# A fixed order for a kernel's first tiles, x sums taken after the transpose, and GpSimd sums in pieces

## The chip, the cores and the metric

The kernel runs on one core of a Trainium2 chip. The time is device microseconds of one execution of the whole program, as the median of several runs; a lower one is better. The core has TensorE (PE, matmuls and transposes), VectorE (DVE), ScalarE (ACT), GpSimd (POOL), and SyncE (SP), which here only issues transfers. Each engine works through a queue of its own in order and waits for others by semaphores.

## The reference

All inputs are float32. x has 2048 rows of 1024.

```python
xn = (x - mean(x)) / sqrt(var(x) + 1e-5)
q, k, v = split(xn @ wqkv)                    # 32 heads of 32 columns each
phi = lambda t: where(t > 0, t + 1, exp(t)) + 1e-6
kv = sum over s of phi(k)[s]^T v[s];  z = sum over s of phi(k)[s]
s = ((phi(q) @ kv) / (phi(q) . z + 1e-6)) @ wo
g = silu((silu(xn @ w1) * (xn @ w3)) @ w2)    # w1, w3: 1024 x 3584; w2: 3584 x 1024
out = x + s * g
```

## The kernel before

Every float32 operand of a matmul is split into two float32r parts: `split` copies the high part on ScalarE (L83) and subtracts it on VectorE (L84). A product takes three matmuls of 128 x 512 per 128 rows of contraction: high x high, high x low, low x high (`mm3`, L92 to L94).

All large products are done in Strassen's form (Winograd's variant): seven products of quarter size in place of eight. The x side needs A11, A12, A22 and four sums S1 to S4 of the quarters, the weight side B11, B21, B22 and T1 to T4. x is taken in two halves h of 1024 rows, each in two chunks of 512 rows; a quarter is a chunk by half the columns.

In the first half, `prepare_first` loads the four tiles (128 rows each, xa) of the first chunk, normalises them, transposes them on TensorE and splits them into A11 and A12. `prepare_rest` loads the tiles xb of the second chunk, takes `moments` (statistics, a square root on ScalarE, and one refining step in small operations), normalises, and forms the sums in `combined`, on GpSimd, 128 x 512 each. The results are written over xa and xb and then transposed and split. Three early groups (keys 0, values 0, keys 1: `gemm` with early=True) multiply B11 with A11 and B21 with A12 before the sums exist. Their whole weights (wk, wv) are loaded into the buffers in which xa lay (tag "raw", two of them), so such a load waits until both tiles of an xa buffer have been transposed for good. Split weights and the fourth tile xb3 share a pool of eight buffers ("b").

While the first half is multiplied (keys, values, queries, then 14 pairs of gate and up with w1 and w3), background jobs run one step per product (`catch_up`): `prepare_next` prepares the second half's x, seven operands of each of four tiles, and stores them to DRAM; after it `weight_sums` forms the T sums of w2 on GpSimd (`sums_of`). The up group's end stores h from GpSimd's queue (L525) and forms the sums of h (`four_sums`), four GpSimd operations of 128 x 256 for each of two chunks, stored to hs_d by SyncE, in the last pair by GpSimd.

The order of instructions on each engine is set when the program is built: a scheduler with its own estimate of time interleaves the streams, within what data, buffers and `tc.issue_after` (a program-order edge behind a given instruction) allow.

Of the kernel before, what the change touches and what calls it, by code (L numbers as in the profile page):

```python
# [16 lines left out]
P = 128  # L17
C = 512
# [4 lines left out]
def tile_linear_attention_times_swiglu(  # L23
# [55 lines left out]
    def split(pair, src, bias=None):  # L79

        hi, lo = pair[:, 0], pair[:, 1]
        if bias is None:
            nc.scalar.copy(out=hi, in_=src)  # L83
            nc.vector.tensor_sub(out=lo, in0=src, in1=hi.bitcast(F32))  # L84
        else:
            nc.scalar.activation(hi, src, AF.Identity, bias=bias)
            nc.vector.scalar_tensor_tensor(lo, src, bias, hi.bitcast(F32), op0=ALU.add, op1=ALU.subtract)
# [36 lines left out]
    def moments(xs, dst):  # L124

        n = len(xs)
        bs = st.tile([P, n, 2, nc.vector.BN_STATS_DIM], F32, tag="bs", name="bs")
        v = st.tile([P, n], F32, tag="v", name="v")
        u = st.tile([P, n], F32, tag="u", name="u")
# [4 lines left out]
        y = dst[:, :, 1]  # L134
        nc.vector.tensor_scalar_add(v, y, 1e-5)
# [11 lines left out]
    def turn_into(A, b, i, name):  # L147

        for n, src in b.items():
            p_ = bank(f"t{n}{name}")  # L150
            for k in range(ND // 2):
                nc.tensor.transpose(p_[:, k * P:(k + 1) * P], src[:, k * P:(k + 1) * P], ident)
            split(A[n][:, :, :, i * P:(i + 1) * P], p_.rearrange("p (k s) -> p k s", k=ND // 2))
# [4 lines left out]
    def prepare_first(A, mom):  # L158

        xs = []  # L160
        for g in range(TH // 4):
            t = load_rows([(2 * g + e) * P for e in range(2)], f"xa{g}")
            for e in range(2):
                i = 2 * g + e
                xs.append(t[:, e])
# [5 lines left out]
    def prepare_rest(A, mom, i, t0):  # L171

        t1 = job_tile([P, D], f"xb{i}") if i < 3 else pb.tile([P, D], F32, tag="b", name=f"xb{i}")
        nc.sync.dma_start(out=t1, in_=x[C + i * P:C + (i + 1) * P, :])
        j = TH // 2 + i
        moments([t1], mom[:, j:j + 1])
        normalise(t1, mom[:, j])
        b = combined(t0, t1, small(f"S1x{i}"))
        yield
        turn_into(A, {n: b[n] for n in ("S2", "S3", "S1", "A22", "S4")}, i, f"0_{i}")  # L180
        yield

    def combined(t0, t1, s1):

        a11, a12, a21, a22 = t0[:, :C], t0[:, C:], t1[:, :C], t1[:, C:]
        nc.gpsimd.tensor_add(out=s1, in0=a21, in1=a22)
        nc.gpsimd.tensor_sub(out=a21, in0=a11, in1=a21)
        nc.gpsimd.tensor_sub(out=a11, in0=s1, in1=a11)
        nc.gpsimd.tensor_sub(out=a12, in0=a12, in1=a11)
        return {"S1": s1, "S3": a21, "S2": a11, "S4": a12, "A22": a22}  # L190

    def prepare_next(i):


        def turn(n, src):
            p_ = bank(f"t{n}1_{i}")
            for k in range(ND // 2):
                nc.tensor.transpose(p_[:, k * P:(k + 1) * P], src[:, k * P:(k + 1) * P], ident)
            o = pb.tile([P, 2, ND // 2, P], FR, tag="b", name=f"{n}o{i}")
            split(o, p_.rearrange("p (k s) -> p k s", k=ND // 2))  # L200
            nc.sync.dma_start(out=a_d[n][:, :, :, i * P:(i + 1) * P], in_=o.bitcast(F32))

        def steps(_):
            t0, t1, t2 = (job_tile([P, D], f"xn{i}_{e}") for e in range(3))
            for c, t in enumerate((t0, t1)):
                r0 = HS + c * C + i * P
                nc.sync.dma_start(out=t, in_=x[r0:r0 + P, :])
# [3 lines left out]
            moments([t0, t1], m)  # L211
            yield True
            yield True
            normalise(t0, m[:, 0])
            yield True
            normalise(t1, m[:, 1])
            yield True
            yield True
            turn("A11", t0[:, :C])
# [728 lines left out]
```

## Time and profile before

| | |
|---|---|
| Time, three runs | 2447.94 us median (2447.08 to 2451.15) |
| The profiled execution's own time | 2447.93 us |
| Its span, first to last instruction | 2446.1 us |
| Mean granted TensorE clock | 0.992 |
| Moved by DMA | 408.12 MB, mean 167 GB/s |
| Chain that ended last | PE 79%, DVE 11%, issue 4%, DMA 4%, ACT 2%, POOL 1% |

The profile is one execution. A line number names the source line that issued an instruction, a tile name the buffer it writes (out<-in), with buffer numbers left out. Busy time of TensorE counts overlapping matmuls once. A wait is the idle time of an engine ahead of an instruction, put down to the instruction that released it.

### The profile page before, as it was taken

What the parts mean: (1) busy time and instruction counts of PE and PEld (TensorE: products, weight loads), DVE (VectorE), ACT (ScalarE), POOL (GpSimd) and SP (SyncE); (2) the same over time, 40 slices, a digit from 0 to 9 for tenths busy, and PEclk for the clock granted to TensorE, in tenths of its full rate; (3) what the DMA queues carried; (4) which work ended last, traced back from release to release, by engine and by line L of the source; (5) the groups of instructions that cost most, each with busy time, mean ns of one, the idle gap of its engine ahead of it and who ended that gap; (6) DMA issues with size and microseconds to landing.
All of it is one profiled execution on the core that took longest, in us unless ns stands there. A gap on an engine that the chain in (4) does not pass through costs nothing.

```text
span 2446.1 us, 31065 instructions
## 1 busy us (share of the span) xinstructions
PE 2358.0 (96%) x10624; PEld 1941.1 (79%) x10624; DVE 1792.1 (73%) x2694; ACT 919.8 (38%) x1648; POOL 724.4 (30%) x873
## 2 busy tenths in 40 slices
PE   5999998999999999999999999999999999999998
PEld 4788887778888888888888888888787788787876
DVE  7654777797777765558878878887745776767798
ACT  4333543323333234445433233323423434343443
POOL 3000122264545310001235552354210032323244
PEclk9999999999999999999999999999999999999999
DMA  3112455575656491124355664566755554454588
GB/s 129 52 52 69 140 170 162 157 257 181 207 173 219 149 345 52 35 78 153 128 196 200 218 227 151 183 230 216 241 157 178 149 156 143 134 153 127 161 277 266
DMA packets 377423, 408.12 MB, mean 167 GB/s; under 512 B 19824, under 2 KB 307568, under 8 KB 377264
## 3 DMA queue, kind: packets, MB, share of 16 engines
q1 hardware_dynamic: 355248, 332.46, 43.2%
q0 software_dynamic: 22016, 73.68, 8.0%
q8 instruction: 83, 1.36, 0.2%
q14 instruction: 76, 0.62, 0.1%
HBM read 268.44 MB, written 137.63 MB: 166 GB/s over the span
## 4 chain that ended last, share of the span: by engine, by line
PE 79%; DVE 11%; issue 4%; DMA 4%; ACT 2%; POOL 1%; SPq 0%; DVEq 0%; ACTq 0%; POOLq 0%
PE dB L92 1%; PE dB L94 1%; PE cB L92 1%; PE dB L93 1%; PE cB L94 1%; PE cB L93 1%; PE kv L415 1%; PE aB L94 1%; PE aB L92 1%; PE aB L93 1%; DMA wpr<-wp_d 1%; DVE acc L865 1%; PE trk L382 1%; DMA rT2B<-wt_d 1%; DMA rA11B<-h_d 1%
## 5 line engine op out<-in xcount | busy, mean ns | idle before, releaser
L474 POOL DMA_DIRECT2D pq_d<-pq x32 | 17.5, 547 | 502.0 <-DVE pq L376 501.9
L525 POOL DMA_DIRECT2D h_d<-sg x112 | 61.5, 549 | 278.5 <-DVE sg L524 257.8
L792 POOL TENSOR_TENSOR acc<-acc,uB 128x512 f32<-128x512 f32 x25 | 41.9, 1676 | 158.4 <-DVE uB L790 158.4
L540 POOL TENSOR_TENSOR w<-w 128x256 f32<-128x256 f32 x28 | 27.8, 992 | 103.5 <-DMA w<-in_B_w 103.5
L509 POOL TENSOR_TENSOR qd<-qd 128x128 f32<-128x128 f32 x32 | 26.6, 832 | 104.2 <-DVE qd L650 100.6
L512 POOL TENSOR_TENSOR hs<-sg,hs 128x256 f32<-128x256 f32 x56 | 54.9, 981 | 2.1
L771 POOL TENSOR_TENSOR acc<-acc,uB 128x512 f32<-128x512 f32 x7 | 11.7, 1666 | 145.8 <-ACT uB L763 145.8
L856 POOL DMA_DIRECT2D s_d<-s x32 | 17.3, 540 | 122.5 <-DVE s L798 64.5
L383 ACT ACTIVATE kvr<-trk 128x512 f32<-128x512 f32 x32 | 19.1, 597 | 77.7 <-PE trk L382 77.5
L510 POOL TENSOR_TENSOR hs<-hs,sg 128x256 f32<-128x256 f32 x56 | 45.9, 820 | 0.0
L511 POOL TENSOR_TENSOR hs<-sg 128x256 f32<-128x256 f32 x56 | 42.8, 765 | 0.0
L509 POOL TENSOR_TENSOR hs<-sg,sg 128x256 f32<-128x256 f32 x56 | 42.0, 749 | 1.1
L92 PE MATMUL cB<-T,XA22B 128*128 128x512 f32 x87 | 35.0, 403 | 6.6 <-DVE acc L796 6.2
L794 POOL TENSOR_TENSOR acc<-acc,uB 128x512 f32<-128x512 f32 x25 | 40.1, 1604 | 0.0
L83 ACT CAST XS4B<-rS4B 128x384 fp32r<-128x384 f32 (+1 forms) x40 | 19.6, 490 | 53.2 <-PE cB L94 45.2
L807 DVE TENSOR_TENSOR acc<-cB,acc 128x512 f32<-128x512 f32 x25 | 17.2, 688 | 30.2 <-PE cB L94 30.2
L84 DVE TENSOR_TENSOR XS1B<-rS1B,XS1B 128x384 fp32r<-128x384 f32 (+1 forms) x40 | 37.2, 931 | 1.7 <-ACT XS1B L83 1.6
L863 ACT ACTIVATE acc<-acc 128x512 f32<-128x512 f32 x32 | 20.2, 632 | 47.2 <-DVE acc L798 14.1
L83 ACT CAST XA11B<-rA11B 128x384 fp32r<-128x384 f32 (+1 forms) x40 | 19.7, 493 | 45.8 <-PE dB L94 28.4
L83 ACT CAST XS1B<-rS1B 128x384 fp32r<-128x384 f32 (+1 forms) x40 | 19.7, 493 | 45.4 <-PE cB L94 26.5
L83 ACT CAST XS3B<-rS3B 128x384 fp32r<-128x384 f32 (+1 forms) x40 | 19.6, 491 | 43.7 <-PE bB L94 15.6
L92 PE MATMUL aB<-B,XA12B 128*128 128x512 f32 x87 | 34.1, 392 | 1.9 <-ACT uB L788 1.6
(5864 smaller groups left out, 8907.8 us busy)
## 6 DMA issues: line engine op xcount, KB each, us to landing
h_d<-sg POOLq DMA_DIRECT2D x112, 256.0 KB, 4.4
hs_d<-hs SPq DMA_DIRECT2D x104, 256.0 KB
qs_d<-qd POOLq DMA_DIRECT2D x32, 512.0 KB, 4.4
w<-in_B_w SPq DMA_DIRECT2D x56, 256.0 KB
wt_d<-w SPq DMA_DIRECT2D x28, 512.0 KB
pq_d<-pq POOLq DMA_DIRECT2D x32, 256.0 KB, 3.0
pqd<-pq_d SPq DMA_DIRECT2D x16, 512.0 KB
S<-a_dS SPq DMA_DIRECT2D x16, 512.0 KB
```

What stands on the lines that cost most here:

```text
L83: nc.scalar.copy(out=hi, in_=src)
L84: nc.vector.tensor_sub(out=lo, in0=src, in1=hi.bitcast(F32))
L92: nc.tensor.matmul(acc, lhsT=wh, rhs=ah, start=start, stop=False, skip_group_check=True)
L93: nc.tensor.matmul(acc, lhsT=wh, rhs=al, start=False, stop=False, skip_group_check=True)
L94: nc.tensor.matmul(acc, lhsT=wl, rhs=ah, start=False, stop=stop, skip_group_check=True)
L509: nc.gpsimd.tensor_add(out=s1, in0=a21, in1=a22)
L510: nc.gpsimd.tensor_sub(out=s2, in0=s1, in1=a11)
L511: nc.gpsimd.tensor_sub(out=s3, in0=a11, in1=a21)
L512: nc.gpsimd.tensor_sub(out=s4, in0=a12, in1=s2)
L525: nc.gpsimd.dma_start(out=h_d[i][2 * h + c][:, 2 * k + n], in_=sg[n, c])
L792: G.tensor_add(out=c22, in0=c22, in1=u)
L794: G.tensor_add(out=c12, in0=c12, in1=u)
```

## The change

1. `moments` has one small operation less, writes the square root to a tile of its own, and takes up to two tiles at a time.
2. `prepare_first` transposes and splits all four tiles of A11 first, then all of A12.
3. The second chunk's tiles are loaded in pairs with their statistics taken per pair (`load_second`). All of that, on each engine, is ordered behind the last split of A12 and behind the GpSimd sums of the tile before, so that the sums run tile by tile.
4. There are four early groups in place of three (values 1 is new), with a buffer of its own for the first group's partial result. The third and the fourth group's second product stand behind the transposes of tiles 0 and 1.
5. `prepare_next` transposes the four quarters and forms the sums from the transposed quarters on VectorE; per tile there are four groups of transposes where there were seven, no GpSimd operation where there were four of 128 x 512, four more VectorE operations and three more ScalarE copies. It needs two row buffers, not three, and 16 steps, not 17.
6. `four_sums` yields after each two operations, and in the first half each half of the sums is stored from GpSimd's queue as soon as it is there. `sums_of` yields after its first two operations, so a background job spreads it over two steps.

```diff
@@ split @@
-            nc.vector.tensor_sub(out=lo, in0=src, in1=hi.bitcast(F32))
+            return nc.vector.tensor_sub(out=lo, in0=src, in1=hi.bitcast(F32))
...
@@ moments @@
-        y = dst[:, :, 1]
-        nc.vector.tensor_scalar_add(v, y, 1e-5)
+        nc.vector.tensor_scalar_add(v, dst[:, :, 1], 1e-5)
         nc.scalar.activation(y, v, AF.Sqrt)
         nc.vector.reciprocal(y, y)
         nc.vector.tensor_mul(u, y, y)
-        nc.vector.tensor_mul(u, u, v)
-        nc.vector.tensor_scalar(u, u, -0.5, 1.5, op0=ALU.mult, op1=ALU.add)
-        nc.vector.tensor_mul(y, y, u)
+        nc.vector.scalar_tensor_tensor(u, u, -0.5, v, op0=ALU.mult, op1=ALU.mult)
+        nc.vector.scalar_tensor_tensor(dst[:, :, 1], u, 1.5, y, op0=ALU.add, op1=ALU.mult)
...
@@ prepare_first @@
-                moments(xs[i:], mom[:, i:i + 1])
+                moments(xs[i:i + 1], mom[:, i:i + 1])
                 normalise(xs[i], mom[:, i])
-                turn_into(A, {"A11": xs[i][:, :C], "A12": xs[i][:, C:]}, i, f"0_{i}")
-        return xs
+                turn_into(A, {"A11": xs[i][:, :C]}, i, f"0_{i}")
+        for i, t in enumerate(xs):
+            _, low = turn_into(A, {"A12": t[:, C:]}, i, f"0_{i}")
+        return xs, low
+
+    def load_second(mom, g):
+        ts = []
+        for i in (2 * g, 2 * g + 1):
+            ts.append(job_tile([P, D], f"xb{i}") if i < 3 else pb.tile([P, D], F32, tag="b", name=f"xb{i}"))
+            nc.sync.dma_start(out=ts[-1], in_=x[C + i * P:C + (i + 1) * P, :])
+        j = TH // 2 + 2 * g
+        moments(ts, mom[:, j:j + 2])
+        return ts
+
+    def prepare_rest(A, mom, i, t0, seconds, behind):
+        with ExitStack() as order:
+            for mark in behind:
+                order.enter_context(tc.issue_after(mark.ins))
+            if i % 2 == 0:
+                seconds += load_second(mom, i // 2)
+            t1, s1 = seconds[i], small(f"S1x{i}")
+            normalise(t1, mom[:, TH // 2 + i])
+            a11, a12, a21, a22 = t0[:, :C], t0[:, C:], t1[:, :C], t1[:, C:]
+            nc.gpsimd.tensor_add(out=s1, in0=a21, in1=a22)
+            nc.gpsimd.tensor_sub(out=a21, in0=a11, in1=a21)
+            nc.gpsimd.tensor_sub(out=a11, in0=s1, in1=a11)
+            last = nc.gpsimd.tensor_sub(out=a12, in0=a12, in1=a11)
+        behind.append(last)
         yield
...
@@ prepare_next, steps @@
-            turn("A11", t0[:, :C])
-            yield True
-            turn("A12", t0[:, C:])
-            yield True
-            b = combined(t0, t1, t2[:, :C])
-            yield True
-            for n in ("A22", "S1", "S3", "S2", "S4"):
+            for n, a in (("A11", a11), ("A12", a12)):
+                p_ = turn(n, a)
+                keep(n, p_)
+                nc.scalar.copy(out=a, in_=p_)
                 yield True
-                turn(n, b[n])
+            p_ = turn("A21", a21)
+            nc.scalar.copy(out=a21, in_=p_)
+            yield True
+            p_ = turn("A22", a22)
+            keep("A22", p_)
+            nc.vector.tensor_add(out=a22, in0=p_, in1=a21)
+            yield True
+            nc.vector.tensor_sub(out=a21, in0=a11, in1=a21)
+            keep("S1", a22)
+            yield True
+            keep("S3", a21)
+            nc.vector.tensor_sub(out=a11, in0=a22, in1=a11)
+            yield True
+            keep("S2", a11)
+            nc.vector.tensor_sub(out=a12, in0=a12, in1=a11)
+            yield True
+            keep("S4", a12)
             yield True
...
@@ half @@
-            xs = prepare_first(A, mom)
-            m = [keys(0, early=True), values(0, early=True), keys(1, early=True)]
-            r = [prepare_rest(A, mom, i, xs[i]) for i in range(TH // 2)]
-            for kind, i in zip("mrrrmmrmrmrmrr", (0, 0, 1, 2, 1, 0, 3, 2, 0, 1, 1, 2, 2, 3)):
-                next({"m": m, "r": r}[kind][i])
+            (xs, low), seconds = prepare_first(A, mom), []
+            behind = [low]
+            m = [f(pair, early=True, own=pair == 0 and f is keys) for pair in range(2) for f in (keys, values)]
+            r = [prepare_rest(A, mom, i, xs[i], seconds, behind) for i in range(TH // 2)]
+            for i in range(4):
+                next(m[i])
+            for i in range(4):
+                next(r[i])
+            next(m[0])
+            next(m[1])
+            for i in (2, 3):
+                with tc.issue_after(next(r[i - 2]).ins):
+                    next(m[i])
+            next(r[2])
+            next(r[3])
...
@@ four_sums @@
         nc.gpsimd.tensor_sub(out=s2, in0=s1, in1=a11)
+        yield
         nc.gpsimd.tensor_sub(out=s3, in0=a11, in1=a21)
         nc.gpsimd.tensor_sub(out=s4, in0=a12, in1=s2)
+        yield
@@ hidden, sums @@
-            four_sums(sg[0, c], sg[1, c], *o)
-            for e in range(2):
-                queue = nc.gpsimd if pair == NF // 2 - 1 else nc.sync
+            for e, _ in enumerate(four_sums(sg[0, c], sg[1, c], *o)):
+                queue = nc.gpsimd if h == 0 or pair == NF // 2 - 1 else nc.sync
                 queue.dma_start(out=hs_d[i][2 * h + c][:, k, e], in_=o[e])
@@ sums_of @@
         nc.gpsimd.tensor_sub(out=b12, in0=b22, in1=b12)
+        yield True
         nc.gpsimd.tensor_sub(out=b22, in0=b22, in1=b11)
```

How this moves instructions shows best in three places. The first is VectorE's queue at the start, from the point at which the first chunk's tile 1 has been normalised (xa: first chunk, xb: second chunk, w0: the early part of a weight, mom: the moments). Before:

```order
L84 TENSOR_TENSOR A12_0_210<-tA120_1_266,A12_0_210 128x4x128
L132 BN_STATS bs_461<-xb3_459 128x6 x2
L142 TENSOR_TENSOR mom_213<-mom_213,u_278 128x1
L142 TENSOR_TENSOR mom_213<-mom_213,u_306 128x1
L84 TENSOR_TENSOR B11k0_1__482<-w0k0_1__480,B11k0_1__482 128x512
L133 BN_AGGR mom_213<-bs_399 128x2
L84 TENSOR_TENSOR B21k0_1__485<-w0k0_1__480,B21k0_1__485 128x512
L137 RECIPROCAL mom_213<-mom_213 128x1 x2
L133 BN_AGGR mom_213<-bs_461 128x2
L145 TENSOR_SCALAR xa1_273<-xa1_273,mom_213 128x1024 x2
```

Now:

```order
L141 TENSOR_SCALAR xa0_214<-xa0_214,mom_213 128x1024
L134 RECIPROCAL y_285<-y_285 128x1
L136 TENSOR_TENSOR u_265<-y_264 128x1
L84 TENSOR_TENSOR A11_0_206<-tA110_0_231,A11_0_206 128x4x128
L136 TENSOR_TENSOR u_286<-y_285 128x1
L137 SCALAR_TENSOR_TENSOR u_265<-u_265,v_263 128x1
L137 SCALAR_TENSOR_TENSOR u_286<-u_286,v_284 128x1
L138 SCALAR_TENSOR_TENSOR mom_213<-u_265,y_264 128x1
L138 SCALAR_TENSOR_TENSOR mom_213<-u_286,y_285 128x1
L141 TENSOR_SCALAR xa1_259<-xa1_259,mom_213 128x1024 x2
```

Before, the normalise of tiles 2 and 3 (the last row) stood behind the statistics of the second chunk and three early weights; now it follows tile 1's with one split between. On SyncE's queue at the same place (names of semaphores in brackets), before:

```order
L174 DMA xb2_397<-in_A_x 128x1024
L261 DMA w0v0_0__418<-in_A_wqkv 128x8x128 [waits DMAHW0_49]
L174 DMA xb3_459<-in_A_x 128x1024 [waits DMAHW1_49]
L261 DMA w0k0_1__480<-in_A_wqkv 128x8x128 [waits DMAHW2_49]
L238 DMA wk0_0__675<-in_A_wqkv 128x8x256 [waits DVE_49,DMAHW3_49,PE_49,Pool_49]
```

Now:

```order
L286 DMA w0v0_0__355<-in_A_wqkv 128x8x128 [waits DMAHW0_49]
L286 DMA w0k0_1__378<-in_A_wqkv 128x8x128 [waits DMAHW1_49]
L286 DMA w0v0_1__401<-in_A_wqkv 128x8x128 [waits DMAHW2_49,DMAHW0_49,DVE_49]
L174 DMA xb3_458<-in_A_x 128x1024 [waits DMAHW3_49,PE_49]
L263 DMA wk0_0__692<-in_A_wqkv 128x8x256 [waits DMAHW4_49,PE_49,Pool_49]
```

The load of xb3 moved behind two more early weights and now waits for TensorE (PE): its buffer is the one that B11 of values 0 held. The second place is GpSimd's queue for the first half's sums (S1x: S1; the number behind S1x, xa, xb: the tile, two tiles to an xa). Before:

```order
L186 TENSOR_TENSOR S1x0_371<-xb0_355 128x512
L186 TENSOR_TENSOR S1x1_392<-xb1_376 128x512
L187 TENSOR_TENSOR xb0_355<-xa0_214,xb0_355 128x512
L187 TENSOR_TENSOR xb1_376<-xa0_214,xb1_376 128x512
L188 TENSOR_TENSOR xa0_214<-S1x0_371,xa0_214 128x512
L186 TENSOR_TENSOR S1x2_413<-xb2_397 128x512
L188 TENSOR_TENSOR xa0_214<-S1x1_392,xa0_214 128x512
L186 TENSOR_TENSOR S1x3_475<-xb3_459 128x512
L189 TENSOR_TENSOR xa0_214<-xa0_214 128x512
```

Now:

```order
L190 TENSOR_TENSOR S1x0_444<-xb0_424 128x512
L191 TENSOR_TENSOR xb0_424<-xa0_214,xb0_424 128x512
L192 TENSOR_TENSOR xa0_214<-S1x0_444,xa0_214 128x512
L193 TENSOR_TENSOR xa0_214<-xa0_214 128x512
L190 TENSOR_TENSOR S1x1_450<-xb1_426 128x512
L191 TENSOR_TENSOR xb1_426<-xa0_214,xb1_426 128x512
L192 TENSOR_TENSOR xa0_214<-S1x1_450,xa0_214 128x512
L193 TENSOR_TENSOR xa0_214<-xa0_214 128x512
```

Four tiles were interleaved; now a tile is finished before the next begins. The third place is GpSimd's queue around the fourth pair's sums of h (hs: those sums, sg: h, w2: a job's weights). Before:

```order
L509 TENSOR_TENSOR hs0_3_0_0_4025<-sg0_3_00_3792,sg0_3_10_3842 128x256
L511 TENSOR_TENSOR hs0_3_0_1_4026<-sg0_3_00_3792 128x256
L543 TENSOR_TENSOR w2_0_1_4103<-w2_0_1_4103 128x256
L512 TENSOR_TENSOR hs0_3_1_1_3993<-sg0_3_11_3778,hs0_3_1_0_3992 128x256
L510 TENSOR_TENSOR hs0_3_0_0_4025<-hs0_3_0_0_4025,sg0_3_00_3792 128x256
L540 TENSOR_TENSOR w2_1_0_4170<-w2_1_0_4170 128x256
L512 TENSOR_TENSOR hs0_3_0_1_4026<-sg0_3_10_3842,hs0_3_0_0_4025 128x256
L540 TENSOR_TENSOR w2_1_1_4281<-w2_1_1_4281 128x256
L541 TENSOR_TENSOR w2_1_0_4170<-w2_1_0_4170 128x256
L541 TENSOR_TENSOR w2_1_1_4281<-w2_1_1_4281 128x256
```

Now:

```order
L546 TENSOR_TENSOR hs0_3_1_0_3948<-sg0_3_01_3786,sg0_3_11_3740 128x256
L549 TENSOR_TENSOR hs0_3_1_1_3949<-sg0_3_01_3786 128x256
L581 TENSOR_TENSOR w2_2_0_4219<-w2_2_0_4219 128x256
L547 TENSOR_TENSOR hs0_3_1_0_3948<-hs0_3_1_0_3948,sg0_3_01_3786 128x256
L564 DMA h_d4_0_88<-sg0_3_10_3807 128x512
L546 TENSOR_TENSOR hs0_3_0_0_3974<-sg0_3_00_3760,sg0_3_10_3807 128x256
L549 TENSOR_TENSOR hs0_3_0_1_3975<-sg0_3_00_3760 128x256
L582 TENSOR_TENSOR w2_2_0_4219<-w2_2_0_4219 128x256
L572 DMA hs_d4_1_109<-hs0_3_1_0_3948 128x512
L550 TENSOR_TENSOR hs0_3_1_1_3949<-sg0_3_11_3740,hs0_3_1_0_3948 128x256
L547 TENSOR_TENSOR hs0_3_0_0_3974<-hs0_3_0_0_3974,sg0_3_00_3760 128x256
L572 DMA hs_d4_1_109<-hs0_3_1_1_3949 128x512
```

Where ten and more sums and weight sums stood in one row, issues of transfers now stand between groups of two to four.

More of the change, by code (lines that the diff above doesn't have):

```diff
@@ L151, in turn_into @@
             for k in range(ND // 2):
-                nc.tensor.transpose(p_[:, k * P:(k + 1) * P], src[:, k * P:(k + 1) * P], ident)
-            split(A[n][:, :, :, i * P:(i + 1) * P], p_.rearrange("p (k s) -> p k s", k=ND // 2))
+                turned = nc.tensor.transpose(p_[:, k * P:(k + 1) * P], src[:, k * P:(k + 1) * P], ident)
+            low = split(A[n][:, :, :, i * P:(i + 1) * P], p_.rearrange("p (k s) -> p k s", k=ND // 2))
+        return turned, low
     def operand_tiles(h):
@@ L171, in prepare_rest @@
[L171 to L178, printed above, removed]
-        yield
[L180 to L190, printed above, removed]
+                turn_into(A, {"A11": xs[i][:, :C]}, i, f"0_{i}")
@@ L457, in half @@
         for pair in range(ND // 2):
[L458 to L461 removed]
+            if h == 0 and pair < 2:
+                run(m[2 * pair])
+                run(m[2 * pair + 1])
+            elif h and pair == 0:
                 side_by_side(keys(pair, paired=True), values(pair, paired=True))
@@ L558, in steps @@
             yield True
-            yield True
-            sums_of(*(t[:, i] for i in range(4)))
+            yield from sums_of(*(t[:, i] for i in range(4)))
             yield True
```

48 lines of the change are left out of this document (24 added, 24 removed).

## The prediction

> **What bounds the kernel now.** I read the page's busy shares and its chain first, then the stretches, then what TensorE waited for.
>
> ```profile
> PE 2358.0 (96%) x10624; PEld 1941.1 (79%) x10624; DVE 1792.1 (73%) x2694; ACT 919.8 (38%) x1648; POOL 724.4 (30%) x873
> ...
> PE 79%; DVE 11%; issue 4%; DMA 4%; ACT 2%; POOL 1%; SPq 0%; DVEq 0%; ACTq 0%; POOLq 0%
> ```
>
> TensorE (PE) is busy 2358.0 us of 2446.1, and 79% of the chain that ended last is its own work. So there are two ways to gain: fewer TensorE instructions, or a share of the 88 us in which it stands. The stretches say where those 88 us lie. A row gives the stretch, its length, then busy time with instruction count for PE, weight load, DVE (VectorE), ACT (ScalarE) and POOL (GpSimd), then granted clock, DMA share, GB/s.
>
> ```profile
> core 0: us, PE busy (x) PEld busy (x) DVE busy (x) ACT busy (x) POOL busy (x), PEclk, DMA share, GB/s
> 0.00:63.30 63.30, 33.57 (x184) 28.82 (x184) 50.30 (x139) 27.26 (x55) 21.72 (x22) 0.96 0.38 125
> ...
> 290.00:560.00 270.00, 252.60 (x1122) 205.43 (x1121) 215.38 (x299) 101.21 (x174) 94.65 (x116) 0.97 0.59 187
> 560.00:1080.00 520.00, 519.84 (x2417) 433.56 (x2416) 351.25 (x505) 177.90 (x306) 149.33 (x189) 1.00 0.47 161
> 1080.00:1740.00 660.00, 650.52 (x2853) 533.20 (x2851) 538.92 (x719) 254.53 (x443) 257.21 (x368) 1.00 0.57 192
> 1740.00:2446.10 706.10, 677.26 (x2944) 551.88 (x2944) 504.12 (x790) 264.50 (x508) 191.84 (x167) 0.99 0.57 175
> ```
>
> Length minus busy: 29.7 us are lost before 63.3, 17.4 in 290 to 560, 0.2 in 560 to 1080, 9.5 in 1080 to 1740, 28.8 after. The change edits the first stretch (start) and the second (the job that prepares the next x); in the third TensorE never waits, so whatever shorter GpSimd runs do there buys nothing. The waits of TensorE (total, times, longest):
>
> ```profile
> PE tA L152 <- DVE xa L145: 21.8, 3, 12.3
> PE bk__696 L92 <- ACT T2k__682 L83: 8.0, 1, 8.0
> ...
> PE ag__4061 L94 <- DVE B21g__4050 L84: 5.2, 1, 5.2
> PE ag__3357 L94 <- DVE B11g__3331 L84: 3.8, 1, 3.8
> PE bg__3380 L92 <- ACT T2g__3339 L83: 2.7, 1, 2.7
> PE bu__3890 L92 <- ACT T2u__3854 L83: 1.8, 1, 1.8
> ```
>
> The first two are all of the start's loss; the other four are 13.5 of the 17.4 in the middle.
>
> **The start.** Rows of the timeline (start, duration):
>
> ```profile
> 14.69 0.80 DVE L145 TENSOR_SCALAR xa<-xa,mom 128x1024 f32<-128x1024 f32 x1
> ...
> 24.87 1.48 DVE L145 TENSOR_SCALAR xa<-xa,mom 128x1024 f32<-128x1024 f32 x2
> ...
> 27.99 3.01 POOL L186 TENSOR_TENSOR S1x<-xb 128x512 f32<-128x512 f32 x2 [26.68 <-DVE xb L145]
> ...
> 29.19 0.79 PE L92 MATMUL ak__341<-A,B11k__334 128*128 128x512 f32 x1
> ...
> 47.12 2.53 POOL L189 TENSOR_TENSOR xa<-xa 128x512 f32<-128x512 f32 x2
> ...
> 49.45 0.38 SPq L238 DMA_DIRECT2D wk__675<-in_A_wqkv  x1
> ...
> 54.72 0.69 DVE L257 TENSOR_TENSOR wk__675<-wk__675 128x512 f32<-128x512 f32 x1 [0.62 <-DMA wk__675<-in_A_wqkv]
> ...
> 63.31 0.79 PE L92 MATMUL bk__696<-S,T2k__682 128*128 128x512 f32 x1 [7.95 <-ACT T2k__682 L83]
> ...
> 63.90 0.68 DVE L84 TENSOR_TENSOR T3k__686<-wk__675,T3k__686 128x512 fp32r<-128x512 f32 x1
> ```
>
> Tiles 2 and 3 of the first chunk are normalised at 24.87 because the second chunk's statistics stand ahead of them in VectorE's queue. In the new order they follow tile 1's normalise (14.69, some 1.2 earlier without a BN_STATS pair ahead of it) after one split and six tiny operations: about 15.6. A11 is then split by about 20 and the first product starts there instead of at 29.19.
>
> That alone gives nothing, since the sums on GpSimd come later. Behind A11, VectorE now has eight splits and six statistics, each some 0.61 from the next (9.2 us over 15 rows, 54.72 to 63.90), so it is busy to about 28.5. The fourth tile, xb3, now lies in the buffer of the second group's B11; its load waits on SyncE until TensorE is done with that product, about 26, and by the weight load above (5.3 from 49.45 to 54.72, for twice the bytes) it lands by 31, I take 30. Behind its statistics on VectorE, a queue in order, wait both pairs' small operations, all four normalises and so all of GpSimd's sums: two statistics (1.2), a normalise (0.8) and, as an estimate, 1.7 for the small square-root chain between them. GpSimd starts at about 33.7 instead of 27.99. Its 16 operations took 21.7 (27.99 to 49.65), 5.4 per tile. Tile by tile, tiles 0 and 1 are done at 44.5, where before xa0 came free only at 49.45: the weight load goes out at 45.0 and lands at 50.3 (54.72 before). From that landing to the T3 split VectorE took 9.2 (54.72 to 63.90) over 15 rows; now there are 13 rows, 7.9, and two of them read two SBUF operands while GpSimd still runs, which I charge 0.5 each. T3 at about 59.2, 4.7 earlier than 63.90.
>
> By then a fourth early group has been multiplied: 24 matmuls, at 0.23 apart (next fence) 5.5 us that no longer come later. Together **-10**. Ends: if GpSimd started at 27.99 as now, 5.7 more, -16; if VectorE's T1 had to wait for the end of GpSimd's sums (55.4 instead of 50.3), -5.
>
> **Fewer transposes.** The job for the next x turned seven blocks per tile and now turns four quarters.
>
> ```profile
> 393.42 0.40 PE L94 MATMUL cu__3212<-A,T4u__3173 128*128 128x512 f32 x1
> 393.65 0.60 PE L198 MATMUL tA<-ident,xn 128*128 128x128 f32 x4
> 394.01 0.48 PE L92 MATMUL du__3213<-S,B22u__3176 128*128 128x512 f32 x1
> 394.33 0.40 PE L93 MATMUL du__3213<-S,B22u__3176 128*128 128x512 f32 x1
> ```
>
> A matmul is 0.23 from the next; with four transposes between, two took 0.91, so a group costs 0.45. Three groups fewer in each of four tiles: 12 x 0.45 = **-5.4**. Where TensorE waits anyway it is worth nothing: 0 is the other end.
>
> **The middle waits.** What holds VectorE there:
>
> ```profile
> 396.78 4.88 DVE L84 TENSOR_TENSOR B11g__3331<-wg__3329,B11g__3331 128x512 fp32r<-128x512 f32 x1
> ...
> 500.42 10.28 DVE L84 TENSOR_TENSOR B21g__4050<-wg__4033,B21g__4050 128x512 fp32r<-128x512 f32 x1
> ...
> 500.47 0.75 POOL L509 TENSOR_TENSOR hs<-sg,sg 128x256 f32<-128x256 f32 x1
> ...
> 508.75 1.39 POOL L543 TENSOR_TENSOR w<-w 128x256 f32<-128x256 f32 x2
> ...
> 590.30 1.07 POOL L543 TENSOR_TENSOR w<-w 128x256 f32<-128x256 f32 x1
> ...
> 590.80 1.11 DVE L257 TENSOR_TENSOR wu__4801<-wu__4801 128x512 f32<-128x512 f32 x1
> ...
> L84 DVE TENSOR_TENSOR S1o<-tS,S1o 128x512 fp32r<-128x512 f32 x4 | 2.7, 685 | 1.9 <-ACT S1o L83 1.9
> ...
> L83 ACT CAST A11o<-tA 128x512 fp32r<-128x512 f32 x3 | 1.7, 583 | 7.5 <-PE tA L198 7.5
> ```
>
> A split takes 685 ns undisturbed. The one at 500.42, with two SBUF operands, took 10.28, exactly as long as GpSimd ran operations end to end (500.47 to 510.14); TensorE's 5.2 hang on it. The one at 396.78 ended with a run of half sums and x sums mixed; 3.8 and 2.7 hang on it. At 590 both alternate at about 1.1: there each GpSimd operation waits for the one before it, and VectorE gets in between. In the new order the x sums are gone from GpSimd here, every half sum is followed by its own store on GpSimd's queue, which waits for the sum, and the 13-operation run of the fourth pair becomes pieces of at most four. So I take the 11.7 us of those three waits as gone. A granted clock of 0.97 over 270 us is 8 us of clock lost, some of it while idle; I take 5, an estimate, for the slow matmuls behind the gaps and 4 of these as gone.
>
> Against it: VectorE gets four additions and subtractions per tile, 16 x 0.685 = 11 us, and ScalarE three copies, 12 x 0.583 = 7 us. VectorE is busy 215 of 270 there and ScalarE 101, so both fit into idle time; but three of the four, and four of the seven splits that follow, now read two SBUF operands and can be held by GpSimd. I charge 3 us of TensorE. Sum **-13**; ends -20 (nearly all idle and slow clock gone) and -3.
>
> The Trainium skill, "SBUF — State Buffer", section "SBUF: two separate sides", says that the pair of ports that VectorE and GpSimd share is locked by whichever instruction starts first, for that whole instruction. By that rule a VectorE operation would wait for one GpSimd instruction, the length of a run would not matter, and the middle would gain only what the x sums' removal gives; the row at 500.42 disagrees, it waited through 13.
>
> **The stores.** 48 half-sum stores move from SyncE's queue to GpSimd's. The nearest rows are the landing time of those already there and the spot where a buffer they read is wanted again:
>
> ```profile
> hs_d<-hs POOLq DMA_DIRECT2D x8, 256.0 KB, 6.0
> ...
> 587.07 1.18 POOL L512 TENSOR_TENSOR hs<-sg,hs 128x256 f32<-128x256 f32 x1
> ...
> 598.44 0.69 DVE L369 TENSOR_TENSOR c12g__4797<-dg__4701,ug__4683 128x512 f32<-128x512 f32 x1 [0.97 <-issue]
> ```
>
> The last sum of a pair ends at 588.25; 0.55 to issue and 6.0 to land makes 594.8, and the buffer is wanted at 598.44: 3.6 us to spare, so cost 0. In parts of 1080 to 1740 the order changes too; I take 0, at most 2 either way of the 9.5 lost there. After 1740 the order is the same. The shorter moments chain saves one tiny operation, 0.
>
> The Trainium skill, same page and section, warns that a transfer issued by GpSimd waits while VectorE holds the shared ports, which a transfer from SyncE does not: a rule against this move. The eight rows with 6.0 us already contain whatever it costs here.
>
> **Sum**: -10 - 5.4 - 13 = -28.4, against the profiled execution's own 2447.93 (its span 2446.1, 1.8 around it), which agrees with the median 2447.94: **2419.5**.
>
> **Rivals.** (A) VectorE becomes the bound in the middle: its 11 us more and the new two-operand reads cost what the broken runs give back. For it: 80% busy; against: 55 us idle and fewer GpSimd operations there. Then -10 and perhaps -2 of the transposes: 2436. (B) The start gives nothing: xb3 lands late, or GpSimd's sums hold T1, and the chain ends as late as now but for the fourth group, which then waits for its own T2: -18.4 alone from the rest, 2429.5. (C) Slower: the stores. If one takes over 9.6 us instead of 6.0 to land, VectorE's add at the spot of 598.44 waits in order with every split behind it, and TensorE with it; 13 pairs times 2.2 us eats the 28, and at 3 us a pair it ends at 2458. For it: GpSimd's queue must also drain its sums ahead of a store; against: the 6.0. (D) The runs do not hold VectorE by their length, so only the x sums' share (3.8 + 2.7) goes: 2426.
>
> **How the numbers follow.** Forecast 0.62, A 0.15, B 0.12, C 0.05, D 0.06. The low end takes -16, -5.4 and -20: 2407. The high end takes -5, 0 and -3: 2440, which holds A, B and D. About what a measurement of this kernel can tell from no change is 0.2%, 4.9 us. Slower than that is C, 0.05; within it the worse half of A with a start at its bad end, 0.07; faster 0.88.
>
> **What would show it.** Right: the T2 wait of bk ends near 59 with 24 more matmuls ahead of it; GpSimd starts near 34, one tile after another; twelve groups of transposes fewer; no VectorE operation over 4 us in 290 to 560, and TensorE idle there under 8 us. Wrong: xb3's statistics waiting beyond 31, TensorE waits on the new subtractions or on splits of S1 to S4, VectorE waiting for a half-sum store, or a loss that grows anywhere in 560 to 1740, where I count none.

## The result, and the profile after

The changed kernel takes 2517.15 us (median of six runs, 2514.31 to 2521.41) against 2448.26 beside it: a ratio of 1.0281, 95% interval 1.0268 to 1.0294. It is 2.8% slower, some 69 us, where 28 us less was forecast. The profiled execution has a span of 2514.5 us, 68.4 more than before.

The stretches of the profile after come first, with the boundaries of the prediction (the first ends where bk begins, 57.62 in place of 63.31):

```profile
0.00:57.62 57.62, 37.91 (x208) 31.79 (x209) 48.96 (x117) 28.57 (x55) 22.97 (x22) 1.00 0.40 128
57.62:290.00 232.38, 224.73 (x1115) 188.34 (x1115) 143.26 (x267) 101.08 (x178) 6.63 (x12) 0.99 0.26 84
290.00:560.00 270.00, 253.56 (x1104) 206.20 (x1104) 218.60 (x308) 105.71 (x179) 95.26 (x129) 0.97 0.59 189
560.00:1080.00 520.00, 516.60 (x2400) 429.41 (x2400) 362.46 (x515) 180.76 (x311) 158.20 (x216) 1.00 0.46 157
...
1310.00:1740.00 430.00, 379.62 (x1583) 307.87 (x1583) 293.29 (x381) 115.70 (x200) 174.31 (x259) 0.94 0.51 170
```

The start is ahead as forecast, and the middle still idles: 16.4 us of 270, where it was 17.4. The loss is in the last row. TensorE stands 50.4 us of 430, and its clock is granted at 0.94, where the kernel before stood 3.8 us in the same stretch:

```profile
1310.00:1740.00 430.00, 426.22 (x1867) 349.27 (x1865) 354.57 (x453) 145.92 (x250) 201.03 (x298) 1.00 0.62 209
```

The starts of the same products say it without fixed boundaries. Here are the T2 products of the gate groups of pair 4 and of the last pair of the second half, before and then after:

```profile
1325.81 0.39 PE L92 MATMUL bg__10676<-S,T2g__10639 128*128 128x512 f32 x1
...
1680.63 0.39 PE L92 MATMUL bg__13644<-S,T2g__13607 128*128 128x512 f32 x1
```
```profile
1313.22 0.39 PE L91 MATMUL bg__10590<-S,T2g__10552 128*128 128x512 f32 x1
...
1738.32 0.39 PE L91 MATMUL bg__13558<-S,T2g__13520 128*128 128x512 f32 x1
```

At pair 4, 12.6 us are still in hand; the last pair is 57.7 behind. So 70.3 us are lost between. Behind it another 10.7 are lost up to the end.

This stretch holds the background work that divides the attention sums (`divide`): a job loads two denominators and two numerators from DRAM, multiplies on VectorE (L688; L650 before), sums on GpSimd and stores to qs_d. The group of that VectorE instruction, in the kernel before and in the changed one (busy, mean ns, then the idle time just before it):

```profile
L650 DVE SCALAR_TENSOR_TENSOR qd<-qd 128x512 f32<-128x512 f32 x32 | 21.8, 682 | 0.0
```
```profile
L688 DVE SCALAR_TENSOR_TENSOR qd<-qd 128x512 f32<-128x512 f32 x32 | 22.3, 696 | 97.1 <-DMA qd<-pq_d 93.5
```

No wait at all before; 97.1 us ahead of the 32 now, 93.5 of them for their own loads from pq_d. One such wait, in the timeline after:

```profile
1331.61 0.56 POOL L691 DMA_DIRECT2D qs_d<-qd  x1
...
1333.50 0.57 POOL L691 DMA_DIRECT2D qs_d<-qd  x1 [0.30 <-POOL qd L550]
...
1334.62 0.54 SPq L680 DMA_DIRECT2D qd<-r_d  x1
...
1339.14 2.13 SPq L682 DMA_DIRECT2D qd<-pq_d  x1
...
1348.16 0.69 DVE L688 SCALAR_TENSOR_TENSOR qd<-qd 128x512 f32<-128x512 f32 x1 [9.21 <-DMA qd<-pq_d]
...
1349.37 0.69 DVE L371 TENSOR_TENSOR c22u__10778<-cu__10746,uu__10724 128x512 f32<-128x512 f32 x1
...
1350.11 0.80 PE L91 MATMUL cu__10746<-A,T4u__10718 128*128 128x512 f32 x1 [4.71 <-DVE c22u__10778 L371]
```

Two jobs store within 2 us of each other (1331.61, 1333.50). Their buffers come free as these stores land, and two jobs are loaded in one go. VectorE, a queue in order, stands at the first of their multiplications for 9.21 us, and behind it stands the addition c22u, which frees the PSUM bank (a part of the memory that matmuls write to) that TensorE's next product needs: 4.71 us. In the kernel before, the multiplications came one at a time, and none of the 32 waited.

That VectorE's queue holds some multiplications too early is seen in its order. Each of the 32 has two figures (the first counts two 256-column slices for each of four chunks, the second the four column blocks k); the first eight:

```
before: 0_0  0_1  0_2  0_3  1_0  1_1  1_2  1_3
after:  0_0  0_2  1_0  0_1  1_2  0_3  2_0  1_1
```

Every second one has moved ahead of one or two that come before it in the program.

### The profile page after: what moved, and what is told of

Same layout as the page of the kernel before. It is cut to its first block, busy times and chain, and to the rows that moved or that the text cites. A ratio compares the mean times of both kernels' runs of the same rounds, so it can differ in the third digit from the quotient of the medians.

```text
span 2514.5 us, 30852 instructions
## 1 busy us (share of the span) xinstructions
PE 2374.8 (94%) x10576; PEld 1947.9 (77%) x10576; DVE 1804.4 (72%) x2688; ACT 926.8 (37%) x1658; POOL 730.0 (29%) x909
## 4 chain that ended last, share of the span: by engine, by line
PE 53%; DMA 9%; DVE 9%; issue 5%; POOL 2%; ACT 1%; SPq 1%; DVEq 0%; POOLq 0%; ACTq 0%
DMA qd<-pq_d 4%; DMA qs_d<-qd 2%; PE dB L93 1%; PE cB L91 1%; PE dB L92 1%; PE dB L91 1%; PE cB L93 1%; PE cB L92 1%; PE aB L93 1%; PE aB L91 1%; PE aB L92 1%; DMA wpr<-wp_d 1%; DMA rS1B<-hs_d 1%; SPq L680 1%; PE kv L442 1%
## 5 line engine op out<-in xcount | busy, mean ns | idle before, releaser
L511 POOL DMA_DIRECT2D pq_d<-pq x32 | 17.4, 545 | 501.2 <-DVE pq L403 461.3
L688 DVE SCALAR_TENSOR_TENSOR qd<-qd 128x512 f32<-128x512 f32 x32 | 22.3, 696 | 97.1 <-DMA qd<-pq_d 93.5
L810 POOL TENSOR_TENSOR acc<-acc,uB 128x512 f32<-128x512 f32 x7 | 11.4, 1623 | 147.8 <-ACT uB L802 147.8
```

## Experiment 1: which part costs the 70 us

A background step runs after each of the first six products of a group, and `tc.issue_after` puts it behind the instructions handed over. A divide takes three steps, so two divides fall into a group, always behind the same two products. The change gave `merge_wo`, which runs ahead of the divides, one step more for each of its four blocks: four steps, one more than a multiple of three. The divides moved from the third and sixth product to the first and fourth. And the first product of a group hands over less than the others:

```python
        copied = nc.scalar.copy(out=u, in_=ba)
        catch_up(copied)                    # after the first product
...
        added = nc.vector.tensor_add(out=u, in0=bb, in1=u)
        catch_up(copied, added)             # after the second
```

Behind the first product no edge holds a VectorE instruction in its place on VectorE, since the only edge is on a ScalarE copy; so the scheduler may move it ahead of its turn, and the order shows that it did. (Why it judged the earlier place to be good, its own estimate of the landing for one, is not shown.) Theory P says that this place is the whole loss. The rivals: S, the merge's sums in two parts keep the job buffers longer; R, the half-sum stores of the second half, now two separate ones on SyncE's queue, hold up the divides' loads.

**merge_whole**: the changed kernel with the merge's sums in one step.

```diff
-                yield from sums_of(*b)
+                for _ in sums_of(*b):
+                    pass
```

> The changed kernel, but the weight sums in merge_wo run in one step as before the change; the split of the sums stays elsewhere. Theory P (place): the extra step per merge moves every later divide by one product mod three, so that every second divide stands behind the first product of a group, where the only edge is on a ScalarE copy, and VectorE's operation is put far ahead of its load; without the extra step the divides go back to their old places, no VectorE wait for a divide's load, and the second half's loss of some 68 us goes: 2437 us (2430 to 2445), since the changed kernel is 10.7 us ahead of the old one at 1334 us. Theory R (the half-sum stores of the second half, now two separate ones on SyncE's queue, hold the divides' loads up): those stores are unchanged here, so 2517 us. Theory S (the sums of the merge in two parts keep the job buffers longer): also 2437 us here.

**one_more_step**: the merge stays split; one empty step more ahead of the attention work.

```diff
         yield from spread_z()
+        yield True
```

> The changed kernel with one empty background step more at the start of the attention work, so the merges keep their split sums, and every divide moves by one product. P: the divides stand behind the second and the fifth product of a group, both with a VectorE edge; 2437 us (2430 to 2450). S and R: the split sums and the split stores are as they were, so 2517 us (2510 to 2525).

**split_merge_alone**: the kernel before, with the merge's sums in two steps (`sums_of` yields in its middle; the sums of w2 still run through in one).

```diff
-                sums_of(*b)
+                yield from sums_of(*b)
```

> The kernel before the change, and only merge_wo's weight sums are spread over two steps (those of w2 stay in one). P: the divides move to the bad places; 2448 + 60 to 70 = 2508 to 2518 us, with VectorE waits for the divides' loads of some 90 us. S: also slower, since the buffers are held longer, 2460 to 2518. R: 2448 us.

**edge**: the changed kernel, with the last VectorE addition of the group before handed over too (second half only).

```diff
-                for m in marks + (tuple(fetched) if in_order else ()):
+                for m in marks + tuple(fetched if in_order else ended):
...
-        nc.vector.tensor_add(out=c12, in0=bd, in1=u)
+        ended[:] = [nc.vector.tensor_add(out=c12, in0=bd, in1=u)]
```

> The changed kernel; in the second half every background step is also ordered behind the last VectorE addition of the group before, so a step behind a group's first product has an edge on VectorE too. No step is added or taken away. P: the divides stay behind products 1 and 4 but run in turn, no VectorE wait for a load over 2 us; 2437 us (2430 to 2450). If the place mattered through something else than the missing edge (what else runs on SyncE or GpSimd there), or by S or R: 2505 to 2520 us.

| kernel | median us | ratio to before | idle ahead of the 32 multiplications |
|---|---|---|---|
| merge_whole | 2446.28 | 0.9996 (0.9986 to 1.0007) | 0.0 |
| one_more_step | 2451.63 | 1.001 (1.0 to 1.0019) | 0.0 |
| split_merge_alone | 2515.66 | 1.028 (1.0264 to 1.0295) | 94.0 |
| edge | 2454.09 | 1.0021 (1.0009 to 1.0033) | 0.0 |

split_merge_alone's row of the group shows the whole loss, made by one step in the kernel before:

```profile
L652 DVE SCALAR_TENSOR_TENSOR qd<-qd 128x512 f32<-128x512 f32 x32 | 22.1, 690 | 94.0 <-DMA qd<-pq_d 80.4
```

P holds for the loss. R falls with merge_whole and split_merge_alone (the stores are as after in one, as before in the other). S falls with one_more_step, where the sums are as split as in the changed kernel, at another place. edge keeps both the split and the place and only adds the edge: its multiplications stand in the order of the program again, and 63 of the 71 us between the changed kernel and merge_whole go. I had expected 2437 of three of these, because the changed kernel is ahead of the old one before the divides; they came out 9 to 17 us above, each beyond the range that I had given under P. So the lead did not reach the end, and the next runs are about that.

## Experiment 2: what the rest of the change is worth

merge_whole, in which the rest of the change works undisturbed, equals the kernel before: 28 us were forecast, none is measured. So each part of the change was put alone into the kernel before: parts 1 to 4 (**start_only**), part 5 (**next_only**), and part 6 without the merge's extra step (**pieces_only**). The core of each is the part's own diff:

```diff
# start_only: parts 1 to 4
+            m = [f(pair, early=True, own=pair == 0 and f is keys) for pair in range(2) for f in (keys, values)]
# next_only: part 5
+            t = [job_tile([P, D], f"xn{i}_{e}") for e in range(2)]
# pieces_only: part 6, but in merge_wo
-                sums_of(*b)
+                for _ in sums_of(*b):
+                    pass
```

> The kernel before the change with its new start alone (A11 first, then A12, sums tile by tile, four early groups, shorter moments); the job for the next x, the half sums, their stores and the weight sums are as before. By the traces the new start was 5 to 10 us ahead at 245 us, a different amount in each execution, and the stretch behind it is unchanged: 2448 - 5 to 10 = 2438 to 2443 us. If the start's gain is given back by what follows (rival of the prediction: the start gives nothing): 2448 us.

> The kernel before the change with the new job for the next x alone. Twelve groups of transposes fewer, 5.4 us, should come off if nothing new waits; by the prediction 3.8 + 2.7 us of waits on mixed runs go too: 2437 to 2443 us. If the 16 more VectorE operations cost what they save (rival A of the prediction): 2446 to 2450 us. No part of it reaches past 560 us except by moving the steps of the jobs behind it.

> The kernel before the change with the sums in pieces alone: half sums two by two, each with its own store, on GpSimd's queue in the first half, w2's weight sums over two steps; merge_wo's sums stay in one step, so the divides stay in place. Theory of the end: with 52 more transfers on GpSimd's queue the drain of GpSimd at the end of the program takes 7.9 us in place of 3.8, as in all four kernels that have these stores, against 3.8 in both that have not: span from the last matmul's start to the end 13.9, not 9.8. The shorter runs take the 5.2 us wait at 505 away: 2448 + 4 - 5 = 2447 us (2443 to 2450). If the drain is due to something else in the change: 9.8 at the end, 2443 us.

And the other way round, merge_whole with the first half's stores back on SyncE's queue, **stores_on_sp**:

```diff
-                queue = nc.gpsimd if h == 0 or pair == NF // 2 - 1 else nc.sync
+                queue = nc.gpsimd if pair == NF // 2 - 1 else nc.sync
```

> The changed kernel with merge_wo's sums in one step again and the half-sum stores of the first half on SyncE's queue, each still right behind its two sums; all else as changed. Theory of the end: 9.8 us from the last matmul's start to the end, 4.1 less than in merge_whole, so 2446.3 - 4.1 = 2442 us (2438 to 2445). If stores on SyncE hold up loads there, or the drain has another cause: 2446 us or more.

| kernel | median us | ratio to before |
|---|---|---|
| start_only | 2448.82 | 0.9999 (0.999 to 1.0008) |
| next_only | 2448.92 | 1.0008 (0.9999 to 1.0017) |
| pieces_only | 2455.25 | 1.0026 (1.0016 to 1.0037) |
| stores_on_sp | 2446.49 | 0.9992 (0.9983 to 1.0001) |

None of the four came out where its main expectation put it. start_only and next_only landed where the gain is given back, pieces_only 5 us above its range. stores_on_sp landed 1.5 us above, although the drain at its end fell to 3.8 us as expected (below).

**The start** gains and loses it again. In start_only bk starts at 58.86, and at 250 us the profile is 6.4 us ahead of the one before. At 382 it is 2.6 behind. Between lies one wait, in this view of TensorE's waits in 280 to 560 of start_only:

```profile
PE bg__3020 L91 <- ACT T2g__2979 L83: 8.1, 1, 8.1
PE ag__4043 L93 <- DVE B21g__4032 L84: 5.2, 1, 5.2
PE ag__3339 L93 <- DVE B11g__3313 L84: 3.8, 1, 3.8
```

The second and third are those of the prediction. The first was 1.2 us before; it is 6.9 of the 9 us given back. In VectorE's timeline of start_only:

```profile
349.26 2.09 DVE L273 TENSOR_TENSOR wg__2969<-wg__2969 128x512 f32<-128x512 f32 x1
351.28 0.68 DVE L130 BATCH_NORM_STATS2 bs<-xn 128x6 f32<-128x512 f32 x1
...
353.08 3.67 DVE L273 TENSOR_TENSOR wg__2969<-wg__2969 128x512 f32<-128x512 f32 x1
356.67 1.21 DVE L84 TENSOR_TENSOR T1g__2975<-wg__2969,T1g__2975 128x512 fp32r<-128x512 f32 x1
...
359.91 0.64 DVE L84 TENSOR_TENSOR T2g__2979<-wg__2969,T2g__2979 128x512 fp32r<-128x512 f32 x1
```

A run of half sums held VectorE here before as well, but then the held instruction was the split of T3, which TensorE wanted a product later:

```profile
361.73 3.71 DVE L84 TENSOR_TENSOR T3g__3001<-wg__2987,T3g__3001 128x512 fp32r<-128x512 f32 x1
```

Now the same run meets the subtractions that make T1 and T2. No code there was edited; with another start the scheduler dealt another order.

**The next x** behaves likewise. The waits in 280 to 560 of the changed kernel:

```profile
PE bg__3012 L91 <- ACT T2g__2976 L83: 6.0, 1, 6.0
PE cg__4026 L91 <- DVE c22g__4056 L371: 3.7, 1, 3.7
PE bq__2498 L91 <- ACT T2q__2461 L83: 3.0, 1, 3.0
PE bu__3856 L91 <- ACT T2u__3819 L83: 2.5, 1, 2.5
```

Of the four named in the prediction only the smallest is still there (bu, 1.8 us then, 2.5 now); others of the same size took the place of the rest. The waits over 0.5 us in that stretch add up to 17.4 before, 19.3 after, 19.4 in next_only, 22.7 in start_only, 16.8 in pieces_only, 18.6 in merge_whole. The one of 6.0 us (bg, ended at 356.8) has new work of the job ahead of it: between 340 and 348 VectorE runs eight of the job's own operations, four additions and subtractions and four splits, among the group's own, ahead of its T1. But two subtractions of the group are also held there, for 2.40 and 2.55 us, so how much of the wait is the job's is not settled.

**The stores** show up where I had not looked: at the very end. The last transfer's issue on GpSimd's queue, in the kernel before (span 2446.1) and after (span 2514.5):

```profile
2441.55 0.54 POOL L866 DMA_DIRECT2D out<-acc  x1 [0.98 <-DVE acc L865]
```
```profile
2505.80 0.54 POOL L905 DMA_DIRECT2D out<-acc  x1 [0.98 <-DVE acc L904]
```

From there to the end it is 4.6 us before and 8.7 after. What fills it in the trace is the drain of GpSimd's sequencer: 3.83 us before, 7.90 after. All kernels with the stores on GpSimd (merge_whole, one_more_step, edge, pieces_only) have 7.9, all without them (split_merge_alone, start_only, next_only, stores_on_sp) 3.8. So the stores cost 4.1 us at the end of every one, though each lands in time. Yet stores_on_sp's median is no lower than merge_whole's. The next table has a possible reason.

**Where the lead goes.** The profiles show more than the medians. The table has the lead over the kernel before at the T2 product of the last gate group of each half, and the time from there, in the second half, to the last matmul (us, one execution each):

| kernel | lead, first half's last pair | lead, second half's last pair | from there to the last matmul |
|---|---|---|---|
| before | 0 | 0 | 755.7 |
| start_only | -0.4 | -0.9 | 756.8 |
| next_only | 3.8 | 3.6 | 759.7 |
| pieces_only | 1.8 | 1.6 | 760.7 |
| merge_whole | 12.3 | 11.6 | 756.6 |
| one_more_step | 10.5 | 10.6 | 766.0 |
| edge | 11.4 | 8.7 | 767.2 |
| stores_on_sp | 7.5 | 5.0 | 761.7 |

So the four kernels that combine the parts do gain 7.5 to 12.3 us in the first half, more than the three parts alone together. one_more_step, edge and stores_on_sp lose all of it behind the last pair, the drain included; merge_whole loses 5.0 us there. Why is open. In merge_whole, pieces_only and stores_on_sp the order of VectorE's and of ScalarE's operations there is that of the kernel before, and yet the stretch took 0.9 to 6.0 us longer. Single executions of one kernel lie up to some 8 us from its median (edge: 2445.94 against 2454.09), and merge_whole's profile (2441.31) is its fastest of ten, so one profile of each cannot tell what is scatter. With the stores on GpSimd the lead in the first half is 3 us and more above that of stores_on_sp; if it is real, it pays for the drain, and the two medians come out alike. That is suggested, not shown.

## Experiment 3: place, number of stores, and the edge in both halves

If place rather than amount decides the middle, empty steps must change it. **shift1** and **shift2** put one and two `yield True` ahead of the job for the next x, on stores_on_sp.

```diff
+        yield True
         yield from go_on([prepare_next(i) for i in range(TH // 2)])
```

> As stores_on_sp, with one empty background step ahead of the job for the next x, so that in the first half every step of that job and of w2's weight sums falls one product later; no operation more. If the place of the steps against the products decides the waits in 280 to 560 us (VectorE's queue in order, six waits of 16 to 20 us in all in each kernel with the new job, the longest of 6 to 7 us at 355 on T2 of the second gate group), that wait changes by several us either way and the time with it: anything from 2436 to 2450 us. If the waits come from the amount of work on VectorE, they stay: 2446 us (2444 to 2449).

> As shift1 with two empty steps. Place: another time in 2436 to 2450 us, with another set of waits in 280 to 560. Amount of work: 2446 us (2444 to 2449).

**few_stores** is merge_whole with only the first four pairs' stores moved.

```diff
-                queue = nc.gpsimd if h == 0 or pair == NF // 2 - 1 else nc.sync
+                queue = nc.gpsimd if h == 0 and pair < 4 or pair == NF // 2 - 1 else nc.sync
```

> As merge_whole, but only the first four pairs' half sums of the first half are stored from GpSimd's queue, 16 stores there in place of 52 more than before the change. GpSimd's drain at the end of the program took 3.83 us with the old number of transfers and 7.90 with 52 more. If it grows with their number: about 5.1 us. If there is a step at some number between: 3.8 or 7.9 us. If it depends on something late in the program: 3.8.

**edge_all** is stores_on_sp with edge's line for both halves.

```diff
-                for m in marks + (tuple(fetched) if in_order else ()):
+                for m in marks + (tuple(fetched) if in_order else ()) + tuple(ended):
```

> As stores_on_sp, and in both halves every background step is also ordered behind the last VectorE addition of the group before. Its order differs little there, since the divides are in place already. 2446 us (2443 to 2449). If steps behind a group's first product float in the first half too, and cost the waits there: 2438 to 2443.

| kernel | median us | ratio to before |
|---|---|---|
| shift1 | 2450.11 | 1.0004 (0.9994 to 1.0013) |
| shift2 | 2447.67 | 0.9993 (0.9984 to 1.0002) |
| few_stores | 2446.30 (one run) | |
| edge_all | 2444.73 | 0.9987 (0.9978 to 0.9996) |

The shifts move the waits by 2 to 3 us (21.8 and 22.0 us in 280 to 560 against 19.4 in stores_on_sp) and the time by 1 to 4. So nothing here separates place from amount in the middle: two other places were no better, which is what the rival expects too. The drain grows with the number of stores: 1.05 us more for the 16 of few_stores (4.88 us), 4.07 more for 52, about 0.07 to 0.08 us each. All are of one size, so number and bytes are not told apart. In the profile of few_stores the lead at the first half's last pair is 9.0 us, where it is 10.5 to 12.3 with all these stores on GpSimd and 5.4 to 7.5 with them on SyncE (stores_on_sp, edge_all and both shifts). edge_all is the only kernel of this document whose whole interval lies below 1: its median is 3 us or 0.13% below that of the kernel before. That is less than the 0.2% that the prediction called the least that can be told from no change, and it lies in the range that I had expected if the edge did nothing there.

## Why the prediction was wrong

**The step that failed** is in the part on the stores: "In parts of 1080 to 1740 the order changes too; I take 0, at most 2 either way of the 9.5 lost there." The term had no reason of its own: one step more in a job shifted the 32 multiplications, every second one to a place with no VectorE edge, VectorE then waited 97.1 us ahead of them, nearly all for their loads, and 0 was 70.3 us. A look at the order of the multiplications, 0_0, 0_2, 1_0, 0_1, would have shown the change of order before any run, though not its price. The prediction did list the outcome as a sign of being wrong: "a loss that grows anywhere in 560 to 1740".

**The start**, -10 forecast: right in the profile after (10.3 ahead at 245 us, T2 at 57.6 where 59 was forecast, GpSimd's first sum at 31.96 where 33.7 was). But in single executions of other kernels with the same start it was 4.7 to 7.7 ahead at 250, and kernels with the old start (split_merge_alone, next_only, pieces_only) were themselves 0.9 to 1.5 ahead of the one profile before. And as a term of the sum it failed: alone it brought nothing (0.9999), because most of the gain was given back in one wait, from about 352 us on. Rival B named that result, for another reason.

**The transposes**, -5.4: twelve groups fewer there are (10624 matmuls and transposes before, 10576 after). Alone, with the rest of the job, they brought nothing that can be measured (1.0008, 0.9999 to 1.0017). The other end that I had named for them, 0, came out in the time. Rival A's reason, that the job's additions and splits on VectorE cost what is saved, is not shown: in next_only's profile 3.8 us of lead do stand at the end of the first half, and they go only behind the last pair of the second.

**The middle waits**, -13: the mechanism (a long run of GpSimd operations holds VectorE) was right, the sum was not. The longest VectorE operation there was 10.28 us, held by 13 GpSimd operations; after the change it is this one (VectorE's timeline, then GpSimd's):

```profile
492.45 3.40 DVE L84 TENSOR_TENSOR B22g__4006<-wg__3982,B22g__4006 128x512 fp32r<-128x512 f32 x1
```
```profile
492.80 0.74 POOL L546 TENSOR_TENSOR hs<-sg,sg 128x256 f32<-128x256 f32 x1
493.50 0.74 POOL L549 TENSOR_TENSOR hs<-sg 128x256 f32<-128x256 f32 x1
494.19 0.73 POOL L582 TENSOR_TENSOR w<-w 128x256 f32<-128x256 f32 x1
494.87 0.56 POOL L572 DMA_DIRECT2D hs_d<-hs  x1
```

The waits that hung on long runs went, but new ones of about the same total came: 18.6 us in merge_whole, where it was 17.4 before. I had charged 3 us for new exposures; in the sum of the waits they ate all of it. The granted clock of the stretch stayed at 0.97 after the change, so the 4 us forecast for it did not come either.

**The stores**: 52 moved, not the 48 that I had counted. In the profile after, the 60 on GpSimd's queue landed in 3.8 us (median; 7.9 at most), where I had taken 6.0 and rival C needs over 9.6. So C as I described it did not happen. Their price, 4.1 us in the drain at the end, was not in the sum.

**The end**: "After 1740 the order is the same" and 0. There 10.7 us were lost: 4.1 are the drain. The other 6.5 us lie between the last gate group and the last matmul: 762.2 us there, 755.7 before, and 756.6 to 767.2 in single profiles of the kernels whose divides run in turn. So it need not come from the divides; that stays open. It is also where the profiles of one_more_step and edge lost most of what they lack against that of merge_whole.

## What to carry to other kernels

Where background work is dealt out one step per product, a step more or less in one job moves every later job against the products; look at which neighbour each moved instruction gets, and above all whether an edge on its own engine still holds it. An in-order engine that reaches an instruction before its load has landed makes everything behind it wait, so a load-dependent instruction wants a fixed place, late enough. And a wait taken away in a scheduled program is only worth what the newly dealt order leaves of it: here three parts with -28 us between them gave nothing in the time, alone or together. Time each part alone before adding up their terms.

## What the runs showed of the hardware

The drain of GpSimd's sequencer at the program's end grew with the number of transfers issued from its queue: 3.83, 4.88 and 7.90 us for 0, 16 and 52 more of 256 KB, although the last of those had landed by about 900 us. A VectorE operation with two SBUF operands stood through three GpSimd operations end to end (3.40 us from 492.45, where 0.69 is its time undisturbed) and ended at 495.85, after GpSimd's queue had turned to issuing the store behind them. The Trainium skill, "SBUF — State Buffer", section "SBUF: two separate sides", says that whichever of the two starts first holds their shared pair of ports for the whole instruction, and the other is blocked. If that is read as a wait for one instruction, the trace disagrees, as at 500.42 in the prediction: the three GpSimd operations took 0.7 us each. What follows on the end of the first, the section does not say.
